# Two layers of decode attention and gated MLP on one core: P times V with P as weights, O turned back in float32, 26 tiles held

## The chip, the core and the metric

The kernel runs on one core of one Trainium2 chip. A core has five engines that run side by side, each with its own instruction queue in program order: TensorE (PE) for matrix products, VectorE (DVE), ScalarE (ACT), GpSimd (POOL) and SyncE (SP), which here only issues transfers from memory (HBM) to the on-chip buffer (SBUF). PE writes into PSUM, eight banks of 128 partitions by 512 float32 columns. An engine waits for another through semaphores. The metric is the device time of one execution in microseconds, lower being better.

## The reference

Four batch rows pass through two identical layers; each is attention over a cache and then a gated MLP. All arrays are bfloat16. B = 4, D = 512, 32 query heads on 8 key/value heads (4 queries share one), 4096 cached positions, head size 128, F = 1792.

```python
def _A_ref(x, k_cache, v_cache, wq, wo):
    q = (x @ wq).reshape(B, Sq, Hq, Dh).transpose(0, 2, 1, 3)
    k = jnp.repeat(k_cache, rep, axis=1)
    v = jnp.repeat(v_cache, rep, axis=1)
    scores = jnp.einsum("bhqd,bhkd->bhqk", q, k) * (Dh ** -0.5)
    p = _softmax(scores, axis=-1)
    o = jnp.einsum("bhqk,bhkd->bhqd", p, v)
    return o.transpose(0, 2, 1, 3).reshape(B, Sq, Hq * Dh) @ wo

def _B_ref(x, w_gate, w_up, w_down):
    g = jnp.einsum("bsd,df->bsf", x, w_gate)
    u = jnp.einsum("bsd,df->bsf", x, w_up)
    return jnp.einsum("bsf,fd->bsd", _sigmoid(g) * u, w_down)

x = A_x
x = x + _A_ref(_layernorm(x), ...); x = x + _B_ref(_layernorm(x), ...)
x = x + _A_ref(_layernorm(x), ...); x = x + _B_ref(_layernorm(x), ...)
```

Both layers use the same weights and the same cache, so a K or V tile that layer 0 has used can be used again by layer 1 if it is still on the chip.

## The kernel before

**Units and pairs.** A unit is one (layer, batch, key/value head): 2 x 4 x 8 = 64. Its K tile and its V tile are 1 MB each, one of 12 slots of SBUF (8 KB in each partition). Two neighbouring heads make a pair; `ORDER` lists the 32 pairs, with those of layer 1 laid between those of layer 0, batch by batch. `RET` names the tiles that stay in their slots from layer 0 to layer 1: 16 K and 12 V, 28 in all. So 48 K and 52 V tiles are loaded, besides 13.25 MB of weights.

**The main loop.** `plan` gives 33 steps; step k does scores and softmax of pair k, and P times V of pair k-1. For each pair:

- `k_turn` (DVE, L871) turns a K tile in place, in blocks, if it was not turned for layer 0.
- `q_blocks` (POOL, L672) lays out the pair's queries with zeros around them, as weights.
- `scores` (PE, L886): a unit takes 16 matmuls with 32 columns of weights and 256 moving columns. Four of them stand on four strips of 32 columns of the array, each writing its own 32 partitions of `S_ps`; both units add into one bank, each in rows of its own, because the other's rows get zero weights.
- `smax`, `spread_max`, `softmax`: row maximum on DVE (L909, L913), spread over the partitions by PE (L920), masked on DVE (L929), exp with running sum on ACT (L937).
- `ptrans`: PE turns P in two matmuls (L982), then ACT copies the result out of `PT` in 16 small pieces (L1005) into `pT`, of which there is one buffer.
- `sums`, `inverse`: the sums over partitions on PE (L960), the reciprocal on DVE (L970).
- `pv` (PE, L1022): V is the weight. A unit takes 32 matmuls, each with a 128x128 block of V as weights and 4 columns of `pT` moving; all add into 4 columns of `O_ps`. So O comes out with the head size on the partitions.
- `normalise` (DVE, L1055) multiplies O with the reciprocals into `oT`; `wo_pair` (PE, L1073; DVE, L1088) multiplies with `wo` and adds to `xT`, for two batches at a time where `partner` allows it.

**A pass.** When a batch ends a layer-0 attention, `pass_steps` lists what leads to its queries of layer 1: LayerNorm, MLP (`wide`, L735; `down`, L818), LayerNorm, q as two row groups (`q_row`, L769), each turned back (`q_half`, L799), then spread (`q_spread`, L647, L658). `PLACES` puts each of the 18 into a step and a place (0 to 8) in that step. Only when all of q is spread can the first pair of layer 1 begin.

**Order on the engines.** Nothing is scheduled by itself: the order of the Python calls is the order of each queue. `FIRST_AT` gives the place at which the first unit's scores of the next pair stand; `STEP` tells when K is turned and whether P times V comes early; `LOADS` orders the loads. `pump` issues every load whose slot is in `free`, on SP's queue; a slot is freed in the program when the last reader was recorded (`scores` or `pv`), and the transfer waits on the chip for that reader. All transfers stand in one queue, in that order.

**The end.** Step 32 does P times V of the last pair, then `wo`, the last LayerNorm and MLP for all four batches at once (`gate_up`, `down_rows`), and the result is written.

Of the kernel before, what the change touches and what calls it, by code (L numbers as in the profile page):

```python
# [5 lines left out]
dt = mybir.dt  # L6
# [9 lines left out]
    {"k": (4, 5, 6, 7), "v": (4, 5, 6, 7)},  # L16
    {"k": (4, 5, 6, 7), "v": (4, 5, 6, 7)},
    {"k": (4, 5, 6, 7), "v": (6, 7)},
    {"k": (3, 5, 6, 7), "v": (6, 7)},
]  # L20

ORDER = [
    (0, 0, (0,)),
    (0, 0, (1,)),
    (0, 0, (2,)),
    (0, 0, (3,)),
    (0, 2, (1,)),
    (0, 1, (1,)),
    (0, 1, (0,)),
    (1, 0, (3,)),  # L30
    (1, 0, (2,)),
    (0, 1, (2,)),
    (0, 1, (3,)),
    (0, 2, (0,)),
    (1, 0, (0,)),
    (1, 0, (1,)),
    (1, 1, (2,)),
    (1, 1, (3,)),
# [3 lines left out]
    (1, 1, (0,)),  # L42
    (0, 3, (0,)),
    (1, 2, (3,)),
    (0, 3, (1,)),
    (0, 3, (2,)),
    (0, 3, (3,)),
# [4 lines left out]
    (1, 3, (2,)),  # L52
    (1, 3, (0,)),
    (1, 3, (1,)),
# [4 lines left out]
        (1, 8), (2, 2), (2, 2), (2, 2), (2, 2), (2, 3),  # L59
        (2, 4), (2, 7), (2, 7), (2, 8), (3, 1), (3, 2),  # L60
        (3, 2), (3, 5), (3, 5), (3, 5), (3, 6), (3, 6),
    ),
    (
        (1, 8), (2, 2), (2, 2), (2, 2), (2, 2), (2, 3),
        (2, 4), (2, 7), (2, 7), (2, 8), (3, 1), (3, 5),
        (3, 5), (3, 5), (3, 5), (3, 5), (3, 6), (3, 6),
    ),
    (
        (1, 8), (2, 2), (2, 2), (2, 2), (2, 2), (2, 3),
        (2, 4), (2, 7), (2, 7), (2, 8), (3, 1), (3, 5),  # L70
        (3, 5), (3, 5), (3, 5), (3, 5), (3, 6), (3, 6),
    ),
    (
        (1, 8), (2, 2), (2, 2), (2, 2), (2, 2), (2, 3),
        (2, 4), (2, 7), (2, 7), (2, 8), (3, 0), (3, 0),
        (3, 0), (3, 0), (3, 2), (3, 2), (3, 5), (3, 6),
# [5 lines left out]
    7, 7, 7, 7, 2, 2, 2, 2,  # L82
    2, 2, 7, 7, 7, 2, 2, 2,
    2, 2, 2, 7, 3, 3, 3, 3,
    3, 3, 7, 7, 7, 7, 7,
# [3 lines left out]
    "kkkk", "kvkv", "kvkv", "vkkv", "kvkv", "kvkv", "kvkv", "vkvk",  # L89
    "kvkv", "kvkv", "kvkv", "kvkv", "kvkv", "kvkv", "kvkv", "kvkv",  # L90
    "kkvv", "kvkv", "kvkv", "kvkv", "kvkv", "kvkv", "kvkv", "vvkk",
    "vkkv", "kvkv", "kvkv", "kvkv", "kvkv", "kvkv", "kvkv", "vv",
# [5 lines left out]
    0, 0, 0, 0, 0, 0, 0, 6,  # L98
    6, 6, 6, 6, 0, 6, 6, 6,
    6, 6, 6, 0, 6, 6, 6, 6,  # L100
    6, 6, 0, 0, 6, 6, 6, 0,
# [105 lines left out]
def bass_interleave_layers__gqa_block_cached__glu_gated_glu__decode_kernel(  # L207
# [17 lines left out]
    P = 128  # L225
# [37 lines left out]
    small = sbt([P, 24], dt.float32, "small")  # L263
# [10 lines left out]
    junk = sbt([P, P], dt.bfloat16, "junk")  # L274

    row_sb = sbt([P, D], dt.bfloat16, "row")
    x_io = row_sb
# [7 lines left out]
    qT_sb = sbt([P, HQ * Bn], dt.bfloat16, "qT")  # L285
    qc_sb = sbt([P, Bn, HKV, NT4, REP], dt.bfloat16, "qc")
    qz_sb = [sbt([P, 2 * NT4, 8 * REP], dt.bfloat16, f"qz{i}") for i in range(2)]
    oT_sb = [sbt([P, HQ, 2], dt.bfloat16, f"oT{i}") for i in range(2)]
    pe_sb = [sbt([P, 2, P], dt.bfloat16, "pe")] * 2
    pT_sb = [sbt([P, XJ, 2, 8, REP], dt.bfloat16, "pT")] * 2  # L290
    rden_2 = sbt([P, 2, 2 * REP], dt.float32, "rden")
    rden_sb = [rden_2[:, i, :] for i in range(2)]
# [6 lines left out]
    QC = [f"qc{b}" for b in range(Bn)]  # L299
    gs_sb = pe_f[:, 0:KF * Bn]  # L300
    t_sb = pe_f[:, 64:64 + KF * Bn]
    hT_bf = qT_sb[:, 0:KF * Bn].rearrange("p (k b) -> p k b", b=Bn)
# [157 lines left out]
    dve(lambda e: e.memset(M_ps[1][:, :], 0.0), writes=["M1"])  # L460

    def head_masks():
# [14 lines left out]
        dve(lambda e: e.tensor_copy(head_b[:, :], head_s), reads=QC, writes=["head"])  # L477
        for u in range(2):
            dve(
                (lambda u: lambda e: e.tensor_scalar(  # L480
                    mask_f[:, :, u, :, :],
                    head_b[:, u * REP:(u + 1) * REP].unsqueeze(1).unsqueeze(1).broadcast_to([P, 4, 4, REP]),
                    1.0, BIG, op0=ALU.subtract, op1=ALU.mult,
                ))(u),
                reads=["head"],
                writes=[f"mask{u}"],
            )
# [125 lines left out]
    def q_mm(nb, h0, h1):  # L613
# [13 lines left out]
        if h1 == HQ:  # L627
            dve(
                lambda e: e.scalar_tensor_tensor(
                    out=qT_sb[:, 0:HQ * nb].rearrange("p (h b) -> p h b", h=HQ),  # L630
# [7 lines left out]
                writes=["qT"],  # L638
            )

    def q_spread(b0, nb):
        N = HQ * nb
        fns = []
        for t in range(NT4):
            for a in range(4):
# [4 lines left out]
                        rhs=qT_sb[:, 0:N],  # L650
# [4 lines left out]
        S.group("pe", fns, reads=["qT"] + IDENT, writes=["M1"])  # L655
        for bi in range(nb):
# [7 lines left out]
                writes=[f"qc{b0 + bi}"],  # L664
            )

    def q_blocks(g):
        _, b, u = seq[2 * g]
        z = g % 2
        S.inst(  # L670
            "pool",
            lambda e: e.tensor_tensor(  # L672
                qz_sb[z][:, :, 0:4 * REP].rearrange("p i (a r) -> p i a r", r=REP),
                qc_sb[:, b, u:u + 2, :, :].rearrange("p u t r -> p (u t) r").unsqueeze(2).broadcast_to([P, 8, 4, REP]),
                blk_f.unsqueeze(1).unsqueeze(3).broadcast_to([P, 8, 4, REP]),
                ALU.mult,
            ),
            reads=[f"qc{b}", "blk"],
            writes=[f"qz{z}"],
        )  # L680
# [82 lines left out]
    def q_row(h):  # L763
        fns = []
        wv = wq_sb.rearrange("p k (h j s d) -> p k h j s d", h=2, j=4, s=4)
        for k in range(KD):
            for st in range(4):
                fns.append(
                    (lambda k, st: lambda e: e.matmul(  # L769
                        M_ps[h][32 * st:32 * st + 1, :],  # L770
# [6 lines left out]
        S.group("pe", fns, reads=["xcb"] + [f"wq{k}" for k in range(KD)], writes=[f"M{h}"])  # L777

    def q_out(h):
        if h == 0:  # L780
            act(
                lambda e: e.activation(row_sb[:, :], M_ps[0][:, :], ACTF.Copy, scale=rs[:, 0:1]),
                reads=["M0", "rs"],
                writes=["row0"],
            )
        else:
            q_half(0)
            dve(
# [565 lines left out]
```

## Time and profile before

| what | us |
|---|---|
| median of three runs (lowest, highest) | 319.17 (318.25, 319.77) |
| the profiled execution, its own time | 319.58 |
| its span, from first to last instruction | 317.6 |
| PE busy with matmuls; with weight loads | 217.4; 162.1 |
| DVE busy | 178.6 |
| ACT busy | 133.7 |
| POOL busy | 25.8 |
| the main transfer queue, share of 16 engines | 93.4% |
| read from HBM | 118.76 MB, 374 GB/s over the span |

The profile is one execution. Busy times of engines overlap, so they do not add up to the span. A group's line names the source line, the engine, what is written and read, the shape (partitions x elements), the count, then the busy time and the mean of one instruction, then the engine's idle time just ahead of these instructions and what ended it. Matmuls overlap one another, so a matmul's own duration is longer than the distance to the next.

### The profile page before, as it was taken

The numbers are of one execution on the slowest core, as the hardware profiler recorded it, in microseconds if no ns is written. First come the engines' busy times: TensorE is split into PE (matmuls) and PEld (weight loads), VectorE is DVE, ScalarE is ACT, GpSimd is POOL, SyncE is SP. The second block draws the span as 40 slices with busy tenths as digits, with TensorE's granted clock in tenths as the row PEclk, the third lists the DMA queues.
The fourth block names the chain that finished last, engine by engine and source line by source line (L and its number), as shares of the span: only waits on it lengthen the run. The fifth ranks groups of instructions, "written<-read, shape, count | busy, mean of one in ns | idle before, by whom it ended". The sixth has DMA issues, their size and how long they took to land. (4 is left out here: it accounts for less than half of the span.)

```text
span 317.6 us, 12066 instructions
## 1 busy us (share of the span) xinstructions
PE 217.4 (68%) x5196; PEld 162.1 (51%) x5196; DVE 178.6 (56%) x449; ACT 133.7 (42%) x588; POOL 25.8 (8%) x106
## 2 busy tenths in 40 slices
PE   1425622224267989687898877779886897888985
PEld 0412412113256557465856545675554576466775
DVE  4487343150556428975742897653877565359343
ACT  0025320304042446765335675541565752367720
POOL 0000000000000001000001100000100000011200
PEclk9999999999999999999996555555555555565555
DMA  7999999999999899999799999999999999999900
GB/s 294 424 423 410 401 405 400 402 396 383 401 415 391 324 355 398 421 424 382 263 372 423 418 418 420 418 420 416 406 421 419 418 420 376 388 354 417 400 18 3
DMA packets 22256, 119.53 MB, mean 376 GB/s; under 512 B 1976, under 2 KB 7868, under 8 KB 8892
## 3 DMA queue, kind: packets, MB, share of 16 engines
q1 hardware_dynamic: 22204, 118.77, 93.4%
q8 instruction: 41, 0.67, 0.8%
q14 instruction: 11, 0.09, 0.1%
HBM read 118.76 MB, written 0.00 MB: 374 GB/s over the span
## 5 line engine op out<-in xcount | busy, mean ns | idle before, releaser
L1005 ACT ACTIVATE pT<-PT 32x64 bf16<-32x64 f32 x496 | 106.3, 214 | 68.2 <-PE PT L982 56.8
L871 DVE STREAM_TRANSPOSE slot<-slot 128x2048 f32<-128x2048 f32 (+1 forms) x61 | 112.1, 1839 | 39.2 <-DMA slot<-in_A_k_cache_dram 39.1
L1022 PE MATMUL O_ps<-pT,slot 128*128 128x4 bf16 x1984 | 61.4, 167 | 30.9 <-DMA slot<-in_A_v_cache_dram 26.9
L886 PE MATMUL S_ps<-slot,qz 128*32 128x256 bf16 x1024 | 65.7, 411 | 17.9 <-DVE slot L871 12.0
L1022 PEld LDWEIGHTS O_ps<-pT,slot 128*128 128x128 bf16 x1984 | 59.4, 105 | 34.8 <-DMA slot<-in_A_v_cache_dram 27.7
L886 PEld LDWEIGHTS S_ps<-slot,qz 128*32 128x32 bf16 x1024 | 30.5, 129 | 35.2 <-DVE slot L871 13.9
L937 ACT ACTIVATE pe<-S_ps,small 128x256 bf16<-128x256 f32 x32 | 15.1, 473 | 50.7 <-issue 29.9
L951 POOL TENSOR_TENSOR small<-small 128x1 f32<-128x1 f32 x64 | 12.3, 193 | 239.4 <-ACT pe L937 236.9
L920 PE MATMUL MS<-ident_bf,small 128*128 128x128 bf16 x64 | 12.5, 298 | 24.1 <-DVE small L913 23.8
L1073 PE MATMUL O_ps<-oT,wo 128*128 128x2 bf16 (+1 forms) x640 | 20.1, 165 | 1.2 <-DVE oT L1055 0.7
L1073 PEld LDWEIGHTS O_ps<-oT,wo 128*128 128x128 bf16 x640 | 18.8, 104 | 2.6 <-DVE oT L1055 2.1
L909 DVE TENSOR_REDUCE small<-S_ps 128x1 f32<-128x256 f32 x32 | 12.7, 398 | 13.0 <-PE S_ps L886 13.0
L920 PEld LDWEIGHTS MS<-ident_bf,small 128*128 128x128 bf16 x64 | 4.2, 110 | 30.9 <-DVE small L913 25.8
L1055 DVE TENSOR_TENSOR oT<-O_ps,rden 128x8 bf16<-128x8 f32 x32 | 5.4, 168 | 25.3 <-PE O_ps L1022 25.0
L672 POOL TENSOR_TENSOR qz<-qc,small 128x128 bf16<-128x128 bf16 x32 | 12.5, 399 | 36.3 <-ACT qc L658 36.3
L929 DVE CUSTOM_DVE_ANT_0 junk<-MS,mask_f,small 128x128 bf16<-128x128 f32 x32 | 10.8, 337 | 7.9 <-PE MS L920 7.7
L769 PE MATMUL M_ps<-wq,xc_bf 128*1 128x512 bf16 x128 | 13.7, 595 | 0.0
L982 PE MATMUL PT<-ident_bf,pe 128*128 128x128 bf16 x64 | 11.9, 288 | 1.3 <-ACT pe L937 1.3
L960 PEld LDWEIGHTS MS<-head_b,small 128*128 128x128 bf16 x96 | 5.1, 107 | 13.0 <-issue 13.0
L658 ACT ACT_TABLE_LOAD x1 | 1.3, 1283 | 21.3 <-PE M_ps L647 21.3
L818 PE MATMUL M_ps<-qT,wd 128*128 128x1 bf16 x224 | 7.0, 166 | 2.7 <-issue 2.7
L818 PEld LDWEIGHTS M_ps<-qT,wd 128*128 128x128 bf16 x224 | 6.8, 105 | 2.9 <-issue 2.9
(86 smaller groups left out, 162.0 us busy)
## 6 DMA issues: line engine op xcount, KB each, us to landing
slot<-in_A_v_cache_dram SPq DMA_DIRECT2D x52, 1024.0 KB, 11.3
slot<-in_A_k_cache_dram SPq DMA_DIRECT2D x48, 1024.0 KB, 11.0
wq<-in_A_wq_dram SPq DMA_DIRECT2D x4, 1024.0 KB, 7.6
wo<-in_A_wo_dram SPq DMA_DIRECT2D x8, 512.0 KB, 16.1
wg<-in_B_w_gate_dram SPq DMA_DIRECT2D x4, 448.0 KB, 13.8
wu<-in_B_w_up_dram SPq DMA_DIRECT2D x4, 448.0 KB, 14.3
wd<-in_B_w_down_dram SPq DMA_DIRECT2D x2, 896.0 KB, 16.5
row<-in_A_x_dram SPq DMA_DIRECT2D x1, 4.0 KB
```

What stands on the lines that cost most here:

```text
L672: lambda e: e.tensor_tensor(qz_sb[z][:, :, 0:4 * REP].rearrange("p i (a r) -> p i a r", r=REP), qc_sb[:, b, u:u + 2, :, :].rearrange("p u ...
L769: (lambda k, st: lambda e: e.matmul(M_ps[h][32 * st:32 * st + 1, :], lhsT=xc_bf[:, k, 0:1], rhs=wv[:, k, h, :, st, :], start=(k == 0), sto ...
L818: (lambda c, k: lambda e: e.matmul(M_ps[0][:, 128 + c * nb:128 + (c + 1) * nb], lhsT=wd_sb[:, k, c * P:(c + 1) * P], rhs=hT_bf[:, k, 0:nb] ...
L871: dve(lambda e: e.transpose(kf, kf), writes=[f"s{st}"])
L886: (lambda t, b2, e_, w0, s: lambda e: e.matmul(S_ps[p][32 * s:32 * s + 8 * REP, 0:2 * P], lhsT=qzf[:, w0:w0 + 8 * REP], rhs=ktv[:, :, s, : ...
L909: lambda e: e.tensor_reduce(m, S_ps[p][:, 0:2 * P], AX.X, ALU.max),
L920: (lambda n, col: lambda e: e.matmul(MS[:, 0:P], lhsT=top(col).broadcast_to([P, P]), rhs=ident_bf[:, :], start=(n == 0), stop=(n == 1)))(n ...
L937: lambda e: e.activation(pe_sb[p].rearrange("p j m -> p (j m)"), S_ps[p][:, 0:2 * P], ACTF.Exp, bias=nm_sb[p], scale=exp_scale, accum_out= ...
L951: (lambda n: lambda e: e.tensor_tensor(sm_sb[p][n + 1], sm_sb[p][n], top(sm_sb[p][n]), ALU.subtract))(n),
L1005: (lambda dst, frm: lambda e: e.activation(dst, frm, ACTF.Copy))(dst, frm),
L1022: (lambda x, c, j: lambda e: e.matmul(O_ps[p][:, ul * REP:(ul + 1) * REP], lhsT=vv[:, x * JG + c * 2 + j, :], rhs=pT[:, x, j, 2 * c + ul, ...
L1073: (lambda c, r: lambda e: e.matmul(O_ps[p][:, 64 + 2 * c:64 + 2 * c + nb], lhsT=wo_sb[:, u * REP + r, c * P:(c + 1) * P], rhs=oT_sb[n][:, ...
```

## The change

P times V changes sides. `pT` gets 16 columns for each of its 32 places: 8 with P of the two 128-column blocks and 4 heads, 8 that stay zero. A unit now takes 16 matmuls: weights are 16 columns of `pT`, the moving operand is 256 contiguous columns of V (two blocks). The four places c go to four strips of `O_ps`, 32 partitions apart. The window of weights of the second unit starts 8 columns earlier, so its P meets other output rows than the first unit's, and both units of a pair add into the same 256 columns of one bank.

```diff
@@ pv
-                for j in range(2):
-                    fns.append(
-                        (lambda x, c, j: lambda e: e.matmul(
-                            O_ps[p][:, ul * REP:(ul + 1) * REP],
-                            lhsT=vv[:, x * JG + c * 2 + j, :],
-                            rhs=pT[:, x, j, 2 * c + ul, :],
-                            start=(x == 0 and c == 0 and j == 0),
-                            stop=(x == XJ - 1 and c == 3 and j == 1),
-                        ))(x, c, j)
-                    )
+                w0 = ((x * 4 + c) * 2 + ul) * 4 * REP - ul * 2 * REP
+                v0 = (x * JG + 2 * c) * DH
+                fns.append(
+                    (lambda x, c, w0, v0: lambda e: e.matmul(
+                        O_ps[p][32 * c:32 * c + 4 * REP, 0:2 * P],
+                        lhsT=pTf[:, w0:w0 + 4 * REP],
+                        rhs=slot[s][:, v0:v0 + 2 * DH],
+                        start=(ul == 0 and x == 0),
+                        stop=(ul == 1 and x == XJ - 1),
+                    ))(x, c, w0, v0)
+                )
```

O now has heads and blocks on the partitions and the head size along the columns, and half of the products (P of one block with V of the other) are not wanted. `o_copy` copies the 256 columns to SBUF in float32 (into the memory of `row_sb`, which q's rows also use), and `o_turn` picks and adds the wanted rows with a 0/1 matrix `sel_f`, in two float32 matmuls, which turns O back.

```diff
+    def o_copy(g):
+        p = g % 2
+        act(
+            lambda e: e.activation(oc_sb[:, :], O_ps[p][:, 0:2 * P], ACTF.Copy), reads=[f"O{p}"], writes=["row0"]
+        )
+
+    def o_turn(g):
...
+                (lambda j: lambda e: e.matmul(
+                    O_ps[p][:, 2 * P:2 * P + 2 * REP],
+                    lhsT=oc_sb[:, j * P:(j + 1) * P],
+                    rhs=sel_f[:, j, :],
+                    start=(j == 0),
+                    stop=(j == 1),
+                ))(j)
+                for j in range(2)
```

In the loop, P's turn of the next pair follows the copy of O directly; O is turned and normalised either at once or at the start of the next step:

```diff
+        for v in pend:
+            o_turn(v)
         if vg is not None:
             sums(vg)
...
         first_turn(0)
+        while pend:
+            normalise(pend.pop())
...
             pv(2 * vg + 1)
             pump()
-            normalise(vg)
+            o_copy(vg)
+            if sg is not None and sg != NP - 1:
+                ptrans(sg)
+            if vg in ends or sg is None or any((k, w) in rows_at for w in (6, 7, 8)):
+                o_turn(vg)
+                normalise(vg)
+            else:
+                pend.append(vg)
```

The way to q in a pass is cut in two halves of 16 heads: row group, `q_out` (ACT for both halves; before, the second was DVE's), `q_turn`, `q_half` (spread and copy), first for the half that the next pair needs (`ahead`), then for the other. `pass_steps` has 20 entries, and a pair of layer 1 needs only its own half. `q_blocks` is two POOL products instead of one, and `qz_sb` is laid out anew:

```diff
-            lambda: q_row(0),
-            lambda: q_out(0),
-            lambda: q_row(1),
-            lambda: q_out(1),
+            lambda: q_row(ha),
+            q_out,
             q_turn,
-            lambda: q_spread(b0, 1),
+            lambda: q_half(b0, ha),
+            lambda: q_row(1 - ha),
+            q_out,
+            q_turn,
+            lambda: q_half(b0, 1 - ha),
```

The masked maximum is written over its input in PSUM (`MS`) instead of a buffer `junk` that is gone. POOL clears `pT` once at the start and a larger part of the last slot near the end. The tables `RET`, `ORDER`, `PLACES`, `FIRST_AT`, `LOADS` and `STEP` are all new; `RET` now holds 17 K and 9 V tiles:

```diff
 RET = [
-    {"k": (4, 5, 6, 7), "v": (4, 5, 6, 7)},
-    {"k": (4, 5, 6, 7), "v": (4, 5, 6, 7)},
+    {"k": (0, 3, 4, 5, 6, 7), "v": (4, 6)},
+    {"k": (5, 6, 7), "v": (4, 5, 6, 7)},
     {"k": (4, 5, 6, 7), "v": (6, 7)},
-    {"k": (3, 5, 6, 7), "v": (6, 7)},
+    {"k": (2, 3, 6, 7), "v": (4,)},
 ]
...
 LOADS = (
-    "kkkk", "kvkv", "kvkv", "vkkv", "kvkv", "kvkv", "kvkv", "vkvk",
...
+    "kkkk", "kkv", "kvkvvk", "kvv", "kkvv", "kvk", "kvvkvv", "kvvk",
...
 STEP = (
-    0, 0, 0, 0, 0, 0, 0, 6,
-    6, 6, 6, 6, 0, 6, 6, 6,
...
+    0, 0, 0, 0, 0, 0, 6, 0,
+    6, 6, 6, 9, 0, 6, 0, 6,
...
```

## The prediction

> **What bounds the kernel now.** I read the page's slices first, then eight long stretches as windows, then the groups by form, then the timeline of the last steps. A "step" is one pass of the main loop (numbered from 0): scores and softmax of pair k, P times V of pair k-1.
>
> The slices: are the transfers busy, and at what clock does PE run.
>
> ```profile
> PEclk9999999999999999999996555555555555565555
> DMA  7999999999999899999799999999999999999900
> GB/s 294 424 423 410 401 405 400 402 396 383 401 415 391 324 355 398 421 424 382 263 372 423 418 418 420 418 420 416 406 421 419 418 420 376 388 354 417 400 18 3
> ```
>
> The DMA engines are full until about 302 us except for dips. The same 32 score matmuls take 1.90 us at 114.83 (a 9 in the clock row) and at 291.50 (a 5): 9s ahead of the first record are no faster clock.
>
> The windows (columns: length, busy time of each engine, granted clock, DMA share, GB/s) size the dips.
>
> ```profile
> core 0: us, PE busy (x) PEld busy (x) DVE busy (x) ACT busy (x) POOL busy (x), PEclk, DMA share, GB/s
> 100.00:124.00 24.00, 20.70 (x455) 14.26 (x455) 9.35 (x36) 11.48 (x51) 1.87 (x7) 1.00 0.94 354
> 124.00:144.00 20.00, 14.83 (x367) 11.14 (x359) 18.16 (x33) 13.03 (x59) 2.21 (x9) 1.00 1.01 420
> 144.00:164.00 20.00, 17.93 (x430) 14.18 (x434) 11.89 (x42) 8.58 (x39) 1.51 (x7) 1.00 0.88 324
> ...
> 264.00:288.00 24.00, 19.46 (x438) 13.52 (x435) 12.38 (x36) 11.32 (x49) 2.26 (x9) 0.57 0.96 372
> ...
> 302.00:318.00 16.00, 11.12 (x339) 10.03 (x336) 6.07 (x33) 2.42 (x11) 0.01 (x1) 0.50 0.02 7
> ```
>
> At 420 GB/s (124 to 144) a unit of 1 MB, 1.049 million bytes, takes 2.5 us. The three low windows are where a batch ends: LayerNorm, MLP and the next q stand between pairs, and slots come free late. Idle transfer time there: (1 - 354/420) x 24 = 3.8, (1 - 324/420) x 20 = 4.6, (1 - 372/420) x 24 = 2.7; together 11 us. Behind 302 nothing is loaded: 16 us of tail. So transfers pace most of the span, and the passes let them idle.
>
> The groups by form give prices (busy, mean ns | idle before).
>
> ```profile
> L1005 ACT ACTIVATE pT<-PT 32x64 bf16<-32x64 f32 x496 | 106.3, 214 | 68.2 <-PE PT L982 56.8
> ...
> L886 PE MATMUL S_ps<-slot,qz 128*32 128x256 bf16 x1024 | 65.7, 411 | 17.9 <-DVE slot L871 12.0 <-POOL qz L672 4.6 <-issue 1.3
> L1022 PE MATMUL O_ps<-pT,slot 128*128 128x4 bf16 x1984 | 61.4, 167 | 30.9 <-DMA slot<-in_A_v_cache_dram 26.9 <-issue 3.4 <-ACT pT L1005 0.2
> ...
> L937 ACT ACTIVATE pe<-S_ps,small 128x256 bf16<-128x256 f32 x32 | 15.1, 473 | 50.7 <-issue 29.9 <-PE O_ps L1022 7.4 <-DVE small L929 7.2
> ...
> L960 PEld LDWEIGHTS MS<-head_b,small 128*128 128x128 bf16 x96 | 5.1, 107 | 13.0 <-issue 13.0
> ...
> L507 PEld LDWEIGHTS M_ps<-xT,small 128*128 128x128 f32 x20 | 5.0, 312 | 4.4 <-DVE xT L1088 1.7 <-DVE sq L576 1.2 <-issue 1.0
> L507 PE MATMUL M_ps<-xT,small 128*128 128x4 f32 x16 | 4.7, 365 | 1.3 <-DVE xT L1088 1.0 <-DVE xT L830 0.3
> ```
>
> The timeline shows a late step, 5.4 us from one turn of P (L982) to the next:
>
> ```profile
> 291.20 0.37 PE L982 MATMUL PT<-ident_bf,pe 128*128 128x128 bf16 x2
> ...
> 291.50 1.90 PE L886 MATMUL S_ps<-slot,qz 128*32 128x256 bf16 x32
> ...
> 291.67 3.80 ACT L1005 ACTIVATE pT<-PT 32x64 bf16<-32x64 f32 x16 [0.70 <-PE PT L982]
> 293.33 0.24 PE L960 MATMUL MS<-head_b,small 128*128 128x8 bf16 x3
> ...
> 293.43 0.99 PE L1073 MATMUL O_ps<-oT,wo 128*128 128x2 bf16 x32
> ...
> 294.39 0.39 PE L920 MATMUL MS<-ident_bf,small 128*128 128x128 bf16 x2
> ...
> 294.58 2.17 PE L1022 MATMUL O_ps<-pT,slot 128*128 128x4 bf16 x64
> ...
> 296.61 0.37 PE L982 MATMUL PT<-ident_bf,pe 128*128 128x128 bf16 x2
> ```
>
> PE has no gap in it, and ACT (pT copies 3.8, exp 0.47, its accumulator read 0.19, and 0.7 to 1.0 idle ahead of the copies) is as long. These last steps are paced by both, with the transfers ending only some 2 us ahead of the last V matmul (304.16).
>
> **The change, part by part.** Counted on the span, 317.6 us; the profiled execution took 319.58, so 2.0 lie around it; the median of the runs is 319.17, 0.4 lower.
>
> *Loads.* Held units go from 28 to 26; by the built order K loads go from 48 to 47, V from 52 to 55. Two more at 2.5 us: **+5.0**. Nothing hides them but idle that is won back. One K turn (2.3 us of DVE) goes away, off the path.
>
> *New tables: idle won back*, between 0 and 11, the whole of it. In the program order I counted, at the end of each step, the MB whose slots are free to load, less the MB that the next step needs. First pass (steps 3, 4, 5): 1, -1, 1 before, 0, -1, 1 after. Second (10, 11, 12): 1, -1, 1, then 2, 0, 2. Third (18, 19): 1, 3 both. Last (24, 25, 26): 3, 1, 3, then 2, 2, 4. So two of four passes have one load (2.5 us) more in hand, at most 5. Half of q is now made ahead of the other half (16 of 32 row matmuls, 1.9 us, leave the chain), but both wide groups of the MLP (1.7 us each) now stand ahead of the spread of the maximum in every pass, and a turn of O is added. I take **-4**.
>
> *P times V.* Before: 64 matmuls of 4 columns, with weights of 128, 27 ns apart: 1.9 us a pair (118.85 to 120.74). After: 32 of 256 columns, four strips side by side. The scores are that shape: 32 in 1.90. The q row (L769, 32 of 512 columns on strips, 3.00 us at 162.64) halved gives 1.5. Between -0.4 and 0 a pair; I take **0**, the scores being the nearer row. The strips then leave PE: at all 32 places where whole-array sums (L960) follow the scores, PE sits 0.41 us, though nothing is awaited. P's turn now follows strips likewise: +0.4 a step on the loop from V to the pT copies; 0 if the wait is something else.
>
> The Trainium skill (TensorEngine Tiling (Array Packing), Key Properties) says that a change of tiling mode drains the array. By the rule entering the strips would cost too, 0.8 a step; by the row, scores start 0.2 behind P's turn, so only leaving does.
>
> *O turned back.* Two float32 matmuls with 128x128 weights. The LayerNorm sum (L507) is one such: two records, 0.59 us, each weight load 0.312. So four records: about 1.0 us of PE a step; 0.66 from below (L1252, eight records with 32-wide weights), 1.2 from above. It stands behind the first scores of the next step, ahead of sums, wo and the spread of the maximum; ACT's exp waits behind them.
>
> *O copied.* 128x256 float32 on ACT, the shape of exp: 0.47. It falls into ACT's idle of 0.7 to 1.0, while P's turn (0.37) runs; 0.1 remains, 0.5 if that idle is gone. Its buffer is the row buffer that q uses, so around q's two rows O is turned at once instead of in the next step.
>
> *Late steps 28 to 31*, now 5.4 each. PE's pieces sum to 1.90 + 0.24 + 0.99 + 0.39 + 1.9 + 0.37 = 5.8, with 0.4 overlapped. Add 1.0 and 0.4: 6.8 with the wo group (steps 30, 31), while a step without it is held by ACT at 5.8. 2 x 1.4 + 2 x 0.4 = 3.6 at most, 0 if the later transfers cover it; the half of q put into step 28 leaves step 27. I take **+2**, little over half.
>
> *Tail.* The last pair gets copy 0.47, a hop 0.2, turn 1.0, a hop 0.1 between V and normalising: 1.8. The turn of the pair before stands ahead of wo: 0.7 of its 1.0 on the path. **+2.5**, from 1.2 to 3.5.
>
> *Fewer PE instructions.* 1,024 matmuls and 1,024 weight loads fewer of 10,392 records. PE holds without a releaser at L1022 come to 5.0 us (2.27 at 264.6); a tenth to a fifth of them: **-0.5**, 0 to -2.
>
> *At no cost.* The clearing of pT on POOL (0.85 us for 896 columns, L1170; here 512, so 0.5) stands ahead of the first q blocks, but loads are 6.8 MB ahead of need there; without that cover 0.5. The longer clearing of the last slot and the second half of the qz products lie in POOL's idle (8% busy). The maximum's mask writing PSUM instead of junk keeps its 0.34 us, within 0.1.
>
> Sum: 5.0 - 4 + 0 + 2 + 2.5 - 0.5 = **+5.0**, 324.6 from the profiled execution, 324.2 from the median: I say 324.
>
> **Rivals.** *PE's clock comes up (faster).* The clock records show full speed twice, for 3.4 us, at 164.9 and 277.6, each time behind 32 q rows in one piece; the rows' step falls from 427 ns to 217 there. V matmuls of 4 columns kept 27 ns in it, so before had nothing to gain; after, V (1.7), P's turn (0.2) and the scores (1.7) make 3.6 us of streaming without a break. If most steps get it, 16 rounds of 213 ns halve: 1.7 us a step, PE's late step falls to 5.1 and costs nothing, a pass (two to three steps) shortens by 3 and 9 of the 11 come back; tail 1.7. 5.0 - 9 + 0 + 1.7 - 0.5 = -2.8, **316**. Against it: 5.4 us of gapless PE at 291 did not raise it, and q's row is now cut in two. It decides from about 2.5 us of streaming in a 3.4 us stretch.
>
> The Trainium skill (TensorE: Matmul & The Clock Gate, Part 1) says the clock is throttled by default and a busy window of about 3.4 us releases it. This case's two stretches agree; whether the new V stream counts as busy no run here shows yet.
>
> *The turn of O paces more than the end.* In each step with a wo group PE is the longest (6.8 against 5.4); slots come free later, the passes win nothing back: 5.0 + 3.6 + 3.5 + 1.5 = 13.6, **332**. For it: PE is busy 3.9 and 4.0 of 4 us in many windows of the passes. Against: between the passes the loads are up to 6 MB ahead of need by the same count.
>
> *A wash.* 7 us of idle come back, the late steps hide behind the two loads, tail +2: 0, **319.5**.
>
> *The strips do not overlap* (the change doesn't do what it says): 32 x 0.213 = 6.8 us a pair, far over 400. The scores' row excludes it; under 1 in 100.
>
> **How the numbers follow.** Forecast 0.43 (321 to 328), clock 0.28, turn of O 0.17, wash 0.12. The time is the forecast's: 324. The range goes down past the clock case's 316, since PE's late step might then fall below ACT's, and up to the turn case: 314 to 332. A measurement tells 0.5%, 1.6 us, from no change: faster 0.28, same 0.12, slower 0.43 + 0.17 = 0.60.
>
> **What would show it.** Loads: 102 K and V issues; GB/s still 420 between passes. Idle: the low windows at 380 or more if won back. V: 32 matmuls in 1.9 us (0.9 if the clock came up; the clock row would hold 9s or 7s in the second half). Turn of O: four records in 1.0 us. Switch: an idle of 0.4 ahead of P's turn. Tail: 18 to 19 us behind the last load. The forecast is wrong if steps 28 to 31 stay at 5.4 us, or if the transfers end ahead of 300 us.

## The result, and the profile after

The changed kernel takes 324.59 us (median of 4 runs, 323.59 to 325.01) against 319.14 in the same comparison (318.25 to 319.77): ratio 1.0147, 95% interval 1.0107 to 1.0186, or +4.7 us at 319.2. The profiled span goes from 317.6 to 322.6. All ratios leave out executions that the chip's slower state disturbed; the profiled one of e4_no_turn_tail, further down, was such a one, so nothing is read from its profile.

The slices of the page of the changed kernel (granted clock, busy share of the DMA engines, what they moved):

```profile
PEclk9999999955556798555557975555877657676555
DMA  7999999999996999999899999999999999999500
GB/s 294 430 419 396 407 412 402 405 385 391 404 393 264 412 417 419 422 419 414 280 365 422 424 419 420 420 413 405 393 423 420 418 424 415 420 419 418 234 2 3
```
Each slice is 8 us. The clock row has 7s, 8s and a 9 among the 5s and 6s of its second half. The dip ahead of 288 us (376, 388, 354 before) has gone and the one around 155 us has narrowed (382, 263 and 372 there before, now 280 and 365). The first pass had 324 and 355 in two slices before; now it has one deep dip, 264 in the thirteenth slice.

The same stretches as windows (length, busy time of each engine, granted clock, DMA share, GB/s):

```profile
core 0: us, PE busy (x) PEld busy (x) DVE busy (x) ACT busy (x) POOL busy (x), PEclk, DMA share, GB/s
96.00:100.00 4.00, 3.40 (x107) 2.92 (x106) 2.94 (x15) 0.27 (x1) 0.00 (x0) 0.50 0.75 291
100.00:124.00 24.00, 19.52 (x461) 13.03 (x453) 12.42 (x42) 15.15 (x64) 2.84 (x12) 0.89 0.93 379
...
144.00:164.00 20.00, 18.12 (x344) 13.23 (x340) 10.39 (x33) 8.90 (x39) 1.32 (x6) 0.50 0.92 354
264.00:288.00 24.00, 21.60 (x454) 14.09 (x455) 14.84 (x49) 13.86 (x58) 2.89 (x12) 0.71 1.01 420
```
At 420 GB/s the idle time of the transfers is (1 - 291/420) x 4 = 1.2 us, (1 - 379/420) x 24 = 2.3, (1 - 354/420) x 20 = 3.1, and none ahead of 288. Two smaller dips are new, 407 GB/s in 164 to 184 and 384 in 224 to 232: 0.6 and 0.7. In all 7.9 us, before 11.3 (0.2 of it in 96 to 100): some 3.4 won back.

The groups by form (busy, mean ns of one | idle before) of the scores, P times V, the turn of O and its copy:

```profile
L924 PE MATMUL S_ps<-slot,qz 128*32 128x256 bf16 x1024 | 56.5, 362 | 10.4 <-DVE oT L1119 4.0 <-DVE slot L909 3.5 <-POOL qz L688 2.9
L1062 PE MATMUL O_ps<-slot,pT 128*16 128x256 bf16 x992 | 55.7, 374 | 22.4 <-DMA slot<-in_A_v_cache_dram 19.9 <-ACT pT L1044 2.0 <-issue 0.4
...
L1090 PE MATMUL O_ps<-sel_f,row 128*128 128x8 f32 x128 | 26.3, 315 | 3.6 <-ACT row L1082 3.6
...
L1082 ACT ACTIVATE row<-O_ps 128x256 f32<-128x256 f32 x32 | 12.3, 384 | 46.2 <-PE O_ps L1062 46.0
```
The scores' mean was 411 ns and is 362 though their number and shape are the same: that is the clock, which was full for 68 us on record here and for 7 before. The turn of O has 128 matmul records, four a step.

The timeline of the last steps, engines PE and ACT (start, us):

```profile
295.57 1.03 PE L1062 MATMUL O_ps<-slot,pT 128*16 128x256 bf16 x16 [0.43 <-DMA slot<-in_A_v_cache_dram]
...
296.54 0.39 PE L1021 MATMUL PT<-ident_bf,pe 128*128 128x128 bf16 x2
...
296.72 0.38 ACT L1082 ACTIVATE row<-O_ps 128x256 f32<-128x256 f32 x1 [1.43 <-PE O_ps L1062]
296.86 1.90 PE L924 MATMUL S_ps<-slot,qz 128*32 128x256 bf16 x32
...
298.69 1.02 PE L1090 MATMUL O_ps<-sel_f,row 128*128 128x8 f32 x4
...
299.56 0.22 PE L998 MATMUL MS<-head_b,small 128*128 128x8 bf16 x3
...
300.05 1.01 PE L1137 MATMUL O_ps<-oT,wo 128*128 128x2 bf16 x32 [0.26 <-DVE oT L1119]
...
302.89 1.03 PE L1062 MATMUL O_ps<-slot,pT 128*16 128x256 bf16 x16
303.00 1.89 ACT L1044 ACTIVATE slot<-PT 32x64 bf16<-32x64 f32 x8 [0.48 <-PE PT L1021]
...
304.91 0.38 ACT L1082 ACTIVATE row<-O_ps 128x256 f32<-128x256 f32 x1
...
305.34 1.02 PE L1090 MATMUL O_ps<-sel_f,row 128*128 128x8 f32 x4 [1.42 <-ACT row L1082]
...
306.70 1.01 PE L1137 MATMUL O_ps<-oT,wo 128*128 128x2 bf16 x32 [0.26 <-DVE oT L1119]
...
307.64 1.89 PE L1062 MATMUL O_ps<-slot,slot 128*16 128x256 bf16 x32
...
309.63 0.38 ACT L1082 ACTIVATE row<-O_ps 128x256 f32<-128x256 f32 x1 [4.34 <-PE O_ps L1062]
...
310.07 1.02 PE L1090 MATMUL O_ps<-sel_f,row 128*128 128x8 f32 x4 [0.55 <-ACT row L1082]
```
Read it from the top. P's turn (L1021) starts as P times V (L1062) ends, without a hole. The turn of O (L1090) stands 1.02 us long between the scores and the sums. Further down, at 302.89, the last pair but one: P times V ends at 303.92, but ACT copies O only at 304.91, behind eight pT copies (L1044), and PE has been idle for 1.42 us when it turns O at 305.34. The last pair's P times V starts at 307.64, though its V had landed at 305.5. Then copy and turn once more, before `wo`.

Loads landed: the last of 102 K and V loads at 305.5 us, before the last of 100 at 303.4. So 2.1 of the 5.0 us of span arose in the transfers (two loads at 2.5 us, less 2.9 won back), and 2.9 behind them: from the last landing to the end it is 17.1 us, before 14.2.

### The profile page after: what moved, and what is told of

It reads as the page before. It is cut to its first block, busy times and chain, and to the rows that moved or that the text cites. A ratio compares the mean times of both kernels' runs of the same rounds, so it can differ in the third digit from the quotient of the medians.

```text
span 322.6 us, 10489 instructions
## 1 busy us (share of the span) xinstructions
PE 225.8 (70%) x4364; PEld 148.1 (46%) x4364; DVE 173.0 (54%) x449; ACT 147.1 (46%) x628; POOL 33.1 (10%) x139
## 4 chain that ended last, share of the span: by engine, by line
PE 37%; DMA 29%; SPq 16%; DVE 10%; issue 4%; ACT 2%; POOL 0%; DVEq 0%; ACTq 0%
DMA slot<-in_A_v_cache_dram 26%; SPq L393 9%; PE O_ps L1062 8%; PE S_ps L924 7%; SPq L407 6%; DVE slot L909 5%; PE O_ps L1090 4%; DMA slot<-in_A_k_cache_dram 3%; PE O_ps L1137 3%; PE M_ps L751 3%; PE M_ps L785 2%; PE M_ps L848 2%; PE M_ps L522 2%; PE MS L958 1%; PE M_ps L597 1%
## 5 line engine op out<-in xcount | busy, mean ns | idle before, releaser
L909 DVE STREAM_TRANSPOSE slot<-slot 128x2048 f32<-128x2048 f32 (+1 forms) x58 | 108.7, 1883 | 31.0 <-DMA slot<-in_A_k_cache_dram 31.0
L1044 ACT ACTIVATE pT<-PT 32x64 bf16<-32x64 f32 x496 | 106.5, 215 | 12.0 <-PE PT L1021 0.7
L1062 PE MATMUL O_ps<-slot,pT 128*16 128x256 bf16 x992 | 55.7, 374 | 22.4 <-DMA slot<-in_A_v_cache_dram 19.9
L924 PE MATMUL S_ps<-slot,qz 128*32 128x256 bf16 x1024 | 56.5, 362 | 10.4 <-DVE oT L1119 4.0
L1062 PEld LDWEIGHTS O_ps<-slot,pT 128*16 128x16 bf16 x992 | 26.5, 110 | 40.8 <-DMA slot<-in_A_v_cache_dram 22.6
L924 PEld LDWEIGHTS S_ps<-slot,qz 128*32 128x32 bf16 x1024 | 27.1, 116 | 24.1 <-DVE slot L909 5.1
L1082 ACT ACTIVATE row<-O_ps 128x256 f32<-128x256 f32 x32 | 12.3, 384 | 46.2 <-PE O_ps L1062 46.0
L1090 PEld LDWEIGHTS O_ps<-sel_f,row 128*128 128x128 f32 x128 | 23.3, 257 | 13.2 <-ACT pT L1044 6.8
L1090 PE MATMUL O_ps<-sel_f,row 128*128 128x8 f32 x128 | 26.3, 315 | 3.6 <-ACT row L1082 3.6
L688 POOL TENSOR_TENSOR qz<-qc,small 128x64 bf16<-128x64 bf16 x64 | 18.6, 294 | 4.7 <-ACT qc L673 1.1
L967 DVE CUSTOM_DVE_ANT_0 MS<-MS,mask_f,small 128x128 f32<-128x128 f32 x32 | 11.1, 348 | 13.8 <-PE MS L958 11.9
L1021 PE MATMUL PT<-ident_bf,pe 128*128 128x128 bf16 x64 | 11.2, 270 | 2.7 <-ACT pe L975 2.5
```

Source lines behind the costliest of these rows:

```text
L688: (lambda ul: lambda e: e.tensor_tensor(qz_sb[z][:, :, 8 * REP * ul:8 * REP * ul + 4 * REP].rearrange("p t (a r) -> p t a r", r=REP), qc_s ...
L909: dve(lambda e: e.transpose(kf, kf), writes=[f"s{st}"])
L924: (lambda t, b2, e_, w0, s: lambda e: e.matmul(S_ps[p][32 * s:32 * s + 8 * REP, 0:2 * P], lhsT=qzf[:, w0:w0 + 8 * REP], rhs=ktv[:, :, s, : ...
L1044: (lambda dst, frm: lambda e: e.activation(dst, frm, ACTF.Copy))(dst, frm),
L1062: (lambda x, c, w0, v0: lambda e: e.matmul(O_ps[p][32 * c:32 * c + 4 * REP, 0:2 * P], lhsT=pTf[:, w0:w0 + 4 * REP], rhs=slot[s][:, v0:v0 + ...
L1090: (lambda j: lambda e: e.matmul(O_ps[p][:, 2 * P:2 * P + 2 * REP], lhsT=oc_sb[:, j * P:(j + 1) * P], rhs=sel_f[:, j, :], start=(j == 0), s ...
```

## The experiments

Twelve kernels, each beside runs of the kernel before on the same chip. Gain or loss is (ratio - 1) x 319.2 us; "landing" and "tail" are the landing of the last K or V load and the time from there to the end, in the profiled execution. Landing, tail and clock come from one execution of each kernel: for e7 its slowest (323.52, median 321.43), for e11 its fastest (317.42, median 318.37).

| kernel | ratio to before (95% interval) | us | loads | landing | tail |
|---|---|---|---|---|---|
| before | 1 | 0 | 100 | 303.4 | 14.2 |
| after | 1.0147 (1.0107 to 1.0186) | +4.7 | 102 | 305.5 | 17.1 |
| e1_old_tables | 1.0493 (1.0429 to 1.0558) | +15.7 | 100 | 311.6 | 20.1 |
| e2_before_26 | 1.0072 (1.0048 to 1.0097) | +2.3 | 102 | 305.6 | 13.5 |
| e3_no_turn | 0.9952 (0.9933 to 0.9970) | -1.5 | 102 | 302.8 | 12.8 |
| e4_no_turn_tail | 1.0080 (1.0049 to 1.0111) | +2.6 | 102 | | |
| e5_bf16_turn | 0.9996 (0.9967 to 1.0025) | -0.1 | 102 | 304.2 | 13.4 |
| e6_old_tables_no_turn | 1.0067 (1.0022 to 1.0112) | +2.1 | 100 | 304.7 | 15.8 |
| e7_new_tables_old_pv | 1.0074 (1.0043 to 1.0104) | +2.4 | 102 | 306.7 | 14.6 |
| e8_held_28 | 1.0328 (1.0277 to 1.0380) | +10.5 | 100 | 308.9 | 19.1 |
| e9_bf16_turn_stream | 1.0246 (1.0202 to 1.0290) | +7.9 | 102 | 310.4 | 16.5 |
| e10_before_stream | 1.0632 (1.0590 to 1.0674) | +20.2 | 100 | 317.2 | 20.6 |
| e11_straight_ends | 0.9974 (0.9946 to 1.0003) | -0.8 | 102 | 301.3 | 14.3 |
| e12_straight_ends_27 | 0.9942 (0.9915 to 0.9970) | -1.9 | 101 | 299.8 | 15.4 |

### The parts: tables, held units, turn

**e1_old_tables.** `RET`, `ORDER`, `LOADS`, `PLACES` and `STEP` of the kernel before in the changed kernel (the 18 places spread over 20).

```diff
-    {"k": (0, 3, 4, 5, 6, 7), "v": (4, 6)},
-    {"k": (5, 6, 7), "v": (4, 5, 6, 7)},
+    {"k": (4, 5, 6, 7), "v": (4, 5, 6, 7)},
+    {"k": (4, 5, 6, 7), "v": (4, 5, 6, 7)},
...
```

> The changed kernel with the tables of before: 28 held units, 48 K and 52 V loads, the old places (the 18 of a pass spread over the 20 that it has now). Loads-and-tail theory (the change costs 5.0 us of loads, wins about 3 us of idle back by its tables, and pays 2.9 us behind the last load for copying and turning O): no extra loads and no idle won, so 319.1 + 2.9 = 322.0 us (321 to 323.5). Rival, the turn of O paces PE in all steps: the passes idle longer as well, 325 us or more. Rival, PE's higher clock shortens the passes: 320 us or less.

+15.7 us, far on the side of the rival. Its windows of two passes:

```profile
144.00:164.00 20.00, 17.83 (x342) 13.12 (x342) 10.08 (x31) 8.78 (x39) 1.31 (x6) 0.50 0.82 299
264.00:288.00 24.00, 20.86 (x400) 14.16 (x404) 11.73 (x44) 9.84 (x40) 0.97 (x4) 0.50 0.93 372
```
299 GB/s where before had 324: with the old tables the new work makes the transfers idle more in this pass (the other window moves 372, as before), and the last load lands 8.2 us later than before, with as many loads. So "two loads and the tail" was not where the time went; the new tables were paying for something large in the passes.

**e2_before_26.** The kernel before, holding two V tiles fewer.

```diff
-    {"k": (4, 5, 6, 7), "v": (4, 5, 6, 7)},
+    {"k": (4, 5, 6, 7), "v": (6, 7)},
```

> The kernel before with two V tiles of batch 0 fewer held (26), nothing else: 102 K and V loads. Up to two loads more are in hand at the first pass (by the count of free slots 3, 1, 3 MB where it was 1, -1, 1 at steps 3, 4, 5). If two loads cost their full 5.0 us wherever they stand: 324.1 us. If the room that they leave wins the first pass's idle (3.8 us) back: 320.3 us. So 320 to 324; near 320 the count of held units alone is not what costs.

+2.3 us where two loads are 5.0: the first pass moves 418 GB/s from 100 to 124 us where before had 354, since loads find free slots there, and half of the price comes back.

**e3_no_turn** and **e4_no_turn_tail.** Copy and turn of O left out, everywhere and for the last two pairs; `normalise` reads O's bank directly.

```diff
         for v in pend:
-            o_turn(v)
...
-            o_copy(vg)
...
-                o_turn(vg)
```

> The changed kernel without copying and turning O: normalising takes columns 0 to 7 of O as they come, so this leaves out the copy and the two float32 matmuls of every pair and the output differs. Loads-and-tail theory: only what lies behind the last load counts, 2.9 us less, 324.6 - 2.9 = 321.7 us, transfers end where they did (305.5). Rival, the turn paces PE in the steps with a wo group and in the passes: 5 us or more less, 319.5 us or below, with the last load landing 2 us or more earlier.

> As the kernel without the turn of O, but left out for the last two pairs alone (30 and 31), whose O is taken unturned; the other 30 pairs are copied and turned. Loads-and-tail theory: the whole of the turn's price lies here, 321.7 us, equal to the kernel without any turn within 0.5. Rival, the turn paces the loop: 1 to 2 us less than the changed kernel for the tail, and the rest only in the kernel without any turn.

Both came out nearer the rival's case (7.1 us less by the medians, and 2.5); without them the kernel is faster than before. Copy and turn cost 1.95% or 6.2 us in all, and at the end 0.67% or 2.1 us; the other 4.1 arise in the loop, 2.7 of them in the transfers (landing 302.8 instead of 305.5).

**e5_bf16_turn.** Copy and selection matrix in bfloat16.

```diff
-    sel_f = sbt([P, 2, 2 * REP], dt.float32, "sel_f")
+    sel_f = sbt([P, 2, 2 * REP], dt.bfloat16, "sel_f")
...
-    oc_sb = row_sb.bitcast(dt.float32)
+    oc_sb = row_sb[:, 0:2 * P]
```

> The changed kernel with O copied and turned back in bfloat16 instead of float32 (two more roundings of O, of the kind that it gets anyway one step later). The turn was four records in 1.02 us; in bfloat16 two, some 0.3. If PE's time in the turn is what costs: most of the 7.1 us that leaving out copy and turn gave, 324.6 - 5 = 319.6 us. If the waits around it cost (copy, two hops, the turn standing ahead of sums and wo): 1 to 2 us less, 323.

319.82 us, the first theory's value; no difference from the kernel before can be told. The turn's group by form:

```profile
L1090 PE MATMUL O_ps<-sel_f,row 128*128 128x8 bf16 x64 | 6.7, 176 | 3.8 <-ACT row L1082 3.8
```
Two records of 176 ns in place of four of 315. The same copy, the same hops, the same place in PE's queue: so of 6.2 us, 4.8 are PE's time in float32, and only 1.4 all the rest, each figure within 1 to 1.5 us.

**e6_old_tables_no_turn** (e1's tables with e3's edit) and **e7_new_tables_old_pv** (the new tables, q in halves, the old form of P times V, on `pT` of the old shape, no copy or turn).

> The changed kernel with the old tables (335.1 us), and without copying and turning O (left out, so the output differs). Turn-in-the-passes theory: with old tables the passes have no slot in hand, so the copy, the turn and their hops between P times V and wo are what delays the loads; without them 322 us or less. Rival, V as the moving operand itself or q in two halves delays the passes: 327 us or more.

> The new tables, 26 held, q in halves, but P times V as before: V as weights, pT 4 columns moving, no copy and no turn. Complete. Against the changed kernel without the turn (317.5 us) it shows what V as the moving operand does by itself. If strips cost their drain of 0.4 us a step: 315 to 316.5 us. If both forms are equal: 317.5. If the higher clock that the moving V brings to PE helps the scores: 319 or more. Below 319.4 it is faster than the kernel before too: the tables alone.

e6: 322.29, at the theory's bound, far from the rival's 327. With the old tables copy and turn cost 13.6 us (15.7 - 2.1), with the new ones 6.2. e7: 321.43, its third case. The new tables alone are no gain, and the moving V without the turn wins 3.9 us (1.22% from e7 to e3). Their groups, first e7 with the old form, then e3 with the moving V:

```profile
L1061 PE MATMUL O_ps<-pT,slot 128*128 128x4 bf16 x1984 | 61.9, 167 | 27.6 <-DMA slot<-in_A_v_cache_dram 23.5 <-issue 2.2 <-ACT pT L1044 1.8
L924 PE MATMUL S_ps<-slot,qz 128*32 128x256 bf16 x1024 | 65.0, 399 | 13.1 <-issue 4.7 <-DVE oT L1118 3.6 <-POOL qz L688 2.5
```

```profile
L1062 PE MATMUL O_ps<-slot,pT 128*16 128x256 bf16 x992 | 58.3, 384 | 31.0 <-DMA slot<-in_A_v_cache_dram 25.2 <-ACT pT L1044 4.3 <-issue 1.2
L924 PE MATMUL S_ps<-slot,qz 128*32 128x256 bf16 x1024 | 57.6, 367 | 13.0 <-DVE oT L1119 6.4 <-POOL qz L688 4.0 <-DVE slot L909 2.7
```
The scores, 65.0 us and now 57.6, are the same matmuls in both. The clock records show full speed for 17 us in e7 and for 55 us in e3. The clock is not all that differs: the time in which PE waited for nothing that the profile shows ("issue", summed over its matmuls) is 14.8 us in e7, 7.4 before and 2.5 in e3. That is the prediction's term of fewer PE instructions. How the 3.9 us divide between it and the clock no run shows.

**e8_held_28.** Two held units back in the new tables.

```diff
-    {"k": (4, 5, 6, 7), "v": (6, 7)},
-    {"k": (2, 3, 6, 7), "v": (4,)},
+    {"k": (1, 4, 5, 6, 7), "v": (6, 7)},
+    {"k": (2, 3, 4, 6, 7), "v": (4,)},
```

> The changed kernel with 28 held units again (K of head 1 of batch 2 and of head 4 of batch 3 held too), nothing else. Two loads fewer are 5.0 us; by the count of free slots the third and fourth passes then have 0 and 1 MB in hand instead of 1 and 2, and steps 13 to 25 one or two less. If the held units alone explain the loss: 319.6 us. If the two slots are worth as much as the loads: 323 to 325.

330.1 us, worse than the worst expectation: two loads fewer, and 5.8 us slower than the changed kernel. A window of the third pass shows a part of it:

```profile
216.00:240.00 24.00, 19.81 (x361) 12.31 (x362) 13.81 (x37) 13.76 (x59) 2.46 (x10) 0.64 0.95 366
```
366 GB/s where the changed kernel moves 407 in the same stretch, or 2.3 us of transfers at 420; there are such dips in other stretches too (370 against 407 in 164 to 184). Two slots were worth 10.8 us here (5.0 + 5.8), twice the loads that they cost.

### Is it the clock, and can one have more of it?

**e9_bf16_turn_stream** and **e10_before_stream.** Eight matmuls of 256 columns a step that nobody reads, in e5's kernel and in the kernel before.

```diff
+    def stream(vg, n):
+        p = vg % 2
+        S.group("pe", [
+            lambda e: e.matmul(
+                O_ps[p][:, 2 * P:4 * P], lhsT=ident_bf[:, :], rhs=wq_sb[:, 0, 0:2 * P], start=True, stop=True
+            )
+        ] * n, reads=IDENT, writes=[f"O{p}"])
...
+        if vg is not None:
+            stream(vg, 4)
         do_wo(wo_ready(k)[:1], (vg + 1) % 2 if vg is not None else k % 2)
...
+            stream(vg, 4)
             pv(2 * vg)
```

> The changed kernel with the turn in bfloat16 (319.8 us) and eight matmuls of 256 moving columns a step whose result nobody reads, four ahead of wo and four ahead of P times V, where PE waits most (for normalise and for V). They only keep PE streaming. If PE's clock is what the moving V brought and what is still to be had: the scores' mean of 363 ns falls to under 300 and the time to 316-318 us. If they are paid in PE time (eight of 109 to 213 ns, 0.9 to 1.7 us a step, some half of it in idle time) while the loads pace: 325 us or more.

> The kernel before with the same eight matmuls a step that nobody reads, nothing else. Its P times V moves 4 columns at a time and its records show full clock in two windows only. If the moving V won its 3.9 us (321.4 to 317.5) by the clock: the clock comes up here too, and the time stays at 319 us or falls below it in spite of the added work. If by the shorter P times V: 325 us or more, at whatever clock.

Both lose, by 8.0 us against e5 and by 20.2. The clock did come up in e9. Its clock row, then the scores and the added matmuls by form:

```profile
PEclk9999875675556795995759996556999767779975
```

```profile
L924 PE MATMUL S_ps<-slot,qz 128*32 128x256 bf16 x1024 | 50.2, 329 | 9.4 <-POOL qz L688 3.4 <-DVE oT L1128 2.4 <-DVE slot L909 1.9
L1018 PE MATMUL O_ps<-wq,ident_bf 128*128 128x256 bf16 x256 | 48.9, 326 | 1.6 <-issue 1.5
```
Full clock for 147 of 294 us on record (68 of 212 in e5), scores at 329 ns (363 in e5). But the added matmuls take 48.9 us of PE. In e10, where the 4-column matmuls lie between, it hardly came up (34 of 230 us), so e10 does not decide between the clock and the shorter P times V, as it was meant to:

```profile
L980 PE MATMUL O_ps<-wq,ident_bf 128*128 128x256 bf16 x256 | 61.8, 392 | 0.0
L886 PE MATMUL S_ps<-slot,qz 128*32 128x256 bf16 x1024 | 61.5, 395 | 12.5 <-DVE slot L871 7.8 <-POOL qz L672 4.8
```
What brings the clock up can be counted. I cut the records at half clock into stretches of 3.41 us (all profiles but e4's) and summed the moving columns that PE took in each, at 213 ns for 256, and a quarter of that for matmuls with at most 32 columns of weights, of which four stand side by side. All 63 stretches with more than 2.63 us were followed by full clock, none of the 433 with less than 2.16 was, and in between it went either way (28 and 51). So the prediction's 2.5 us is borne out. By this count the 64 matmuls of 4 columns of a pair, 1.9 us of PE, are 0.2 us.

So the higher clock is real and worth having where work that is needed anyway brings it; work done for the clock alone costs more than it brings.

**What one microsecond of PE is worth.** I closed each block of consecutive records of scores, P times V, turn of O and added matmuls (gaps under 0.15 us) and summed the blocks from 90 us on. Five kernels have the same tables and the same 26 units:

| kernel | P times V | scores | turn | added | sum | us against before |
|---|---|---|---|---|---|---|
| e3 | 52.4 | 46.8 | 0 | 0 | 99.2 | -1.5 |
| e5 | 50.4 | 45.4 | 6.1 | 0 | 101.9 | -0.1 |
| e7 | 56.4 | 53.8 | 0 | 0 | 110.2 | +2.4 |
| after | 49.6 | 45.7 | 23.6 | 0 | 118.9 | +4.7 |
| e9 | 40.3 | 39.8 | 6.0 | 41.8 | 127.9 | +7.9 |

From e3 to e9 it is 9.4 us of time for 28.7 us of PE, 0.33 each, and a straight line between the two puts the other three at -0.6, +2.1 and +5.0, each within its interval. Among these five, whether the PE time is a turn, an old P times V or idle matmuls makes no difference that can be told. Where it stands does: e11 (below) has the same tables and units and 105.8 us by this count, the line puts it at +0.7, and it measured -0.8 (-1.7 to +0.1). With the old tables and 28 held units the price is higher: 0.44 from before to e10 (46.3 us more of PE in the same groups), 0.52 from e6 to e1 (97.0 to 123.4). And PE's time is not all: e6 has 13.5 us less of it than before (110.5), with the tables and 28 units of before, and is 2.1 us slower. So something else in the change costs time with the old tables, q in halves and its places perhaps; no run shows which.

### A version that beats both

**e11_straight_ends.** e5's kernel, with the last pair of each batch and layer in the old form (V as weights, read from the new `pT`), with no copy and no turn.

```diff
+    straight = ends | {NP - 1}
...
+            if g in straight:
+                for c in range(4):
+                    for j in range(2):
+                        fns.append(
+                            (lambda x, c, j: lambda e: e.matmul(
+                                O_ps[p][:, 2 * P + ul * REP:2 * P + (ul + 1) * REP],
+                                lhsT=vv[:, x * JG + c * 2 + j, :],
+                                rhs=pT[:, x, 2 * c + ul, j * REP:(j + 1) * REP],
...
-            for c in range(4):
+            for c in range(0 if g in straight else 4):
```

> The changed kernel with the turn in bfloat16, and the last pair of each batch and layer (eight pairs of 32) by the old form of P times V, V as weights, with no copy and no turn: there the copy, turn and hops stand between P times V and a pass. Complete. If what is left of the turn's price (319.8 against 317.5 without it) sits at these ends: 317.5 to 318.5. If it is spread over all steps, or the old form's longer P times V takes it back: 319.5 to 320.5.

318.37 us, in the first range, but its interval reaches 1.0003 and overlaps e5's. In the profile the loads land 2.9 us earlier than in e5, while the tail is 0.9 longer.

**e12_straight_ends_27.** The last pair but one in the old form too, and K of head 1 of batch 3 held (shown against e11).

```diff
-    {"k": (2, 3, 6, 7), "v": (4,)},
+    {"k": (1, 2, 3, 6, 7), "v": (4,)},
...
-    straight = ends | {NP - 1}
+    straight = ends | {NP - 2}
...
-            o_turn(v)
+            if v not in straight:
+                o_turn(v)
```

> The version with the turn in bfloat16 and the old form at the eight ends (318.4 us), with the last pair but one in the old form too and one unit more held (27: K of head 1 of batch 3). Complete. With the turn mostly gone the transfers of that version show no gap over 0.7 us after 108 us, so a slot in hand is worth less and a held unit should be worth its load again: 2.5 us less, and some 0.4 from the last pair but one: 315.5 to 316.5 us. If the slot is still worth as much as the load: 318.5 or more.

317.17 us, ratio 0.9942 (0.9915 to 0.9970): 0.6% faster than the kernel before, and by the two ratios 2.0% faster than the changed one. That is less than the 315.5 to 316.5 expected. What it moved over its span, in slices:

```profile
GB/s 292 425 424 399 410 401 409 410 388 380 408 407 303 419 397 421 420 417 419 386 406 421 423 419 416 422 415 421 419 417 415 398 424 417 421 417 416 264 4 3
```
The first pass still has its dip (303), the second a small one (386); from there on no slice is under 398 until the loads end. The held unit's load came back in part: the last landing is 1.5 us earlier than e11's, and the tail 1.1 longer: steps 28 to 31, from one exp to the next, take 6.4, 6.4, 7.3 and 5.6 us, as long as in e11 (6.4, 6.4, 7.1 and 5.8), though the loads land earlier. How much of the 1.1 us between e11 and e12 is the held unit and how much the pair in the old form was not told apart; their intervals overlap.

## Why the forecast came true, and where its sum was right by errors that cancel

The time was forecast at 324.0 and came out at 324.6. Four groups of terms, as the runs price them (each measured figure within 1 to 1.5 us):

| term | forecast | measured | from |
|---|---|---|---|
| loads and new tables (+5.0, -4) | +1.0 | +2.4 | before to e7 |
| P times V, fewer instructions (0, -0.5) | -0.5 | -3.9 | e7 to e3 |
| copy and turn in the loop (late steps +2) | +2.0 | +4.1 | e4 less e3 |
| copy and turn in the tail | +2.5 | +2.1 | after less e4 |
| sum | +5.0 | +4.7 | |

The measured groups follow one another from before to after, so their sum must be the whole; only the single ones say something. P times V was taken 3.4 us too dear, tables and loop 1.4 and 2.1 too cheap. The direction and the price of the end were reasoned rightly; that the total came within 0.6 us was luck. The range, 314 to 332, held the times of the three rivals at 316, 319.5 and 332 as well.

*Loads and tables.* 102 loads, as counted, and the last one 2.1 us later. The direction was right: two loads, less idle won back. The reason given for the idle was too narrow. The term "idle won back" was priced as a property of the tables, but it depends on what stands in the passes: the same tables with the old P times V gained nothing (e7 and e2, +2.4 and +2.3), and with the turn of O they and the two units let go are worth 11.0 us (e1 to after). The counting of slots showed where (two of the four passes had a load more in hand), not how much.

*P times V.* The size was the failing: 0 from the row of the scores, measured -3.9. The row was right (32 in 1.89 us at half clock, as the timeline shows at 307.64); what the step left out is that the moving V raises the clock for the scores as well. The term of fewer PE instructions, -0.5, is in this group too; its 5.0 us of PE holds at L1022 was the weight loads' idle, PE's own row there has 3.4. P times V fell by 4.0 us of PE from e7 to e3 and the scores by 7.0. The clock was kept as a rival, all or nothing: "If most steps get it". It came for 68 of 264 us on record, and belonged in the sum. The Trainium skill (TensorE: Matmul & The Clock Gate, Part 1: The HAM clock gate) has a busy window of about 3.4 us release the throttle; the stretches of either clock on record here are whole multiples of 3.41 us, but for the last, which the end of the run cuts; that agrees, and the new V stream does count as busy. PE without a gap was not enough: before had none over 0.02 us for 11.0 us from 241.24 on, and stayed at half clock.

*The strips' drain, +0.4 a step,* does not exist. The 0.41 us ahead of the sums was idle of the weight loads only; in the timeline before, the sums' first matmul (293.33) starts as the scores end (291.50 + 1.90). I took the weight loads' idle for PE's. After, P's turn at 296.54 starts within the modelled end of P times V. The Trainium skill (TensorEngine Tiling (Array Packing), Key Properties) says that a change of mode drains the array; no row here shows a pause of PE for it, in either direction.

*O turned back.* Four records, 1.02 us at half clock: as worked out from the LayerNorm sum; at full clock it was 0.61. The copy took 384 ns where 470 were taken.

*Late steps.* +2 was forecast for steps 28 to 31. From the start of one exp to the next they took 6.84, 6.11, 4.83 and 7.22 us against 5.36, 5.68, 5.08 and 5.41, +3.5 and so close to the upper bound of 3.6; from one turn of P to the next, the prediction's own mark, 6.29, 5.61, 6.02 and 6.03 against 5.52, 5.41, 5.41 and 4.91, +2.7. Not all of it is the turn: without it (e3) the same steps still take 23.3 us by exp, 1.7 less than the 25.0. But the turn cost in the passes as well, which the step had put among what the tables win net: leaving out copy and turn brought the last landing forward by 2.7 us.

*Tail.* 2.1 us measured by leaving it out, 2.9 by the profile, 2.5 forecast, and for the reasons given: copy, turn and hops of the last pair, the turn of the pair before ahead of `wo`. One wait was not foreseen: the copy of the pair before stands behind eight pT copies on ACT, 1.42 us of idle PE.

*The rivals.* The clock rival occurred in part, as told. "The turn of O paces more than the end" (written 332; its 13.6 us on 319.2 are 332.8) named what the 4.1 us in the loop are, but not their size with the new tables; with the old ones it came in full, at 335.1, and with 28 units held at 330.1. That the change was no disaster hangs on the tables and on the two units let go. The strips overlapped, as the scores' row said.

*What would have made it wrong:* neither late steps at 5.4 us nor transfers that end ahead of 300 us were seen. Of its other signs, the low windows came to 379, 354 and 420 GB/s where 380 was to show idle won back, and the tail to 17.1 us behind the last landing, where 18 to 19 were named (before, by the same mark, 14.2).

## What to carry to other kernels

Where transfers pace and slots are few, an engine that is "hidden" still has a price: here a third of a microsecond of time for each microsecond of PE on average over five kernels with the same tables, and about half with the old tables and 28 units held. So price added work on every engine that frees slots, not at the end alone; and when a sum of several terms comes out right, test the groups singly before believing them. A form of matmul with many moving columns can pay, here 3.9 us, and raise the clock for its neighbours; a float32 turn gave that gain back, and a bfloat16 one cost about a quarter as much (1.4 of 6.2 us).

## What the runs showed of the hardware that was not expected

- The clock reacts to the columns that PE moves, not to PE being busy: it came up behind every stretch of 3.41 us with more than 2.63 us of them, and never behind less than 2.16. With V moving, full clock for 68 us on record (55 without the turn); with 4 columns moving, 7 us before and 17 us in e7. Eight added matmuls of 256 columns a step gave 147 us in e9 but 34 us in e10, beside the 4-column form.
- 9s in the clock row ahead of the first clock record are not measured: before's records start at 164.9 us and after's at 61.1, and before's scores ran at half clock under a 9 (1.90 us for 32 at 114.83).
- Two float32 matmuls with 128x128 weights are four records and occupied 0.81 us a step on average (23.6 us in 29 steps); the same two in bfloat16 0.21.
